# A gated mix of a spectral filter and an MLP: shorter products of zeros at the start, one operation and one transfer at the end

## The chip, the cores and the metric

The kernel runs on one core of a Trainium2 chip. The metric is the device time of one execution in microseconds (us); three runs of the kernel before took 353.65, 354.13 and 354.32 us. A profile of one execution shows what each engine did: PE (TensorE; its weight loads are listed as PEld), DVE (VectorE), ACT (ScalarE), POOL (GpSimd) and SP (SyncE, which issues most transfers). ACT and POOL issue transfers too.

## The reference

x is 2048 x 512. The result is `g * a + (1 - g) * b`, where all three come from x:

```python
g = sigmoid((x * gate_w).sum(-1, keepdims=True))
X = rfft2(x) * (w_r + 1j * w_i)      # w: 2048 x 257
a = irfft2(X, s=(2048, 512))
h = gelu(x @ w1 + b1)                # w1: 512 x 1792
b = h @ w2 + b2                      # w2: 1792 x 512
```

## The kernel before

The rows of x are taken as 16 sets of 128 (`j`), the hidden columns as 14 blocks of 128 (`f`), the output columns as 4 blocks of 128 (`q`). The 16 sets are worked on four at a time (`c`), so that one block of a result is 128 x 512.

The Fourier transform over the 512 columns is a product with tables of cosines and sines (`pd`, plain f32, `forward`), that over the 2048 rows a product of 128 (`py`) with butterflies on VectorE (`stage1`, `filt`, `stage4`); the way back is `pz` and `pa` (`inverse`). In the MLP numbers are split into two parts of 12 bits, high and low, and a product is three products in one pass each (type fp32r); sevenfold products of 2 x 2 blocks (`seven`, `down_seven`) save an eighth of them. `nu` and `ux` are the products with w1, `po` those with w2, `dx`, `dm`, `dn`, `dz` and `dl` the last ones with w2, in `down_seven`. `ph` are the first products with w1, of which the first take raw x and w1 in plain f32.

Each piece of work is a `Step` with an engine, and the order of all 2146 steps is written out in the list `ORDER`; each engine executes its own steps in that order. A second list, `SLOTS`, says for each of the 900 buffers, in the order in which the steps name them, which slot of its pool it lies in. `w` is a pool of 46 blocks of 128 x 512, `ps` are the 8 banks of PSUM, `t2k`, `ttab` and others are further pools. A buffer whose slot was held by another has to wait until that one's last reader is done; these waits are made from the order and the slots.

At the start (lines 499 to 515) VectorE sets `zero` (128 x 128, `w`, fp32r), and PE multiplies it with itself `WARM` = 9 times (`warm`, line 506), into the bank `none`, which nobody reads; the moving side repeats `zero` four times to make 512 columns. Three more products of 256 columns (`FILL`) stand between later steps. All products are issued on line 420, which is `mm`, so they are told apart by their tiles' names. The first loads of x are issued by ACT and SP. `cf`, the table of the first transform, gets four further columns on VectorE (line 547) before the first `pd`.

At the end (`down_seven`, line 1051, with `out_of`, line 1066) the eight blocks of 128 x 512 of the last two `c` are taken out of PSUM and stored. The very last one is split: `dl` k = 0 and k = 1, 256 columns each, both filled by VectorE (`plus`) and then by nine products, of which PE does those of k = 0 first. Each is copied by ACT with scale -1 into a tile `t`. For k = 0 this is one ACT operation, and SP stores it in one transfer. For k = 1 it is two ACT operations of 128 columns; the first half is stored by SP, the second by ACT itself.

## Time and profile before

| | us |
|---|---|
| median of three runs | 354.13 (353.65 to 354.32) |
| the profiled execution | 353.74 |
| its span, from the first to the last instruction | 352.0 |
| PE busy | 344.8 (98%) |
| DVE busy | 333.4 (95%) |
| ACT busy | 301.6 (86%) |
| POOL busy | 56.6 (16%) |

Busy time of PE is modelled from pipelined products that overlap, so its share says that PE always had something under way, not that it ran at its peak. The profile's chain of waits goes back from the last instruction to whatever released it; its share by engine says what set the time. A product's own duration contains its way through the array, so what one costs in a row of many is the time from its start to the next one's start. In merged rows, this is the stretch less the duration of the last one.

### The profile page before, as it was taken

The page shows a single profiled execution, that of the slowest core. Times are in us where ns is not written, and L with a number is a line of the kernel's source. Part 1 is how long each engine was busy: PE and PEld are TensorE (multiplying, and loading weights), DVE is VectorE, ACT ScalarE, POOL GpSimd, SP SyncE. Part 2 cuts the span into 40 slices and gives each one's busy share as a digit, 9 for nine tenths or more (in the row PEclk, how much of TensorE's full clock was granted, in tenths as well). Part 3 has the DMA queues.
Part 4 walks back from the last instruction along what each step waited for, and adds up shares of the span by engine and source line. Part 5 has one row for each costly group of instructions (what it writes and reads, how often), then busy time and mean ns, then how long its engine had stood idle before and what let it go on. Part 6 is the DMA issues. An engine that isn't in the chain of part 4 may idle for free.

```text
span 352.0 us, 5796 instructions
## 1 busy us (share of the span) xinstructions
PE 344.8 (98%) x1742; PEld 291.9 (83%) x1742; DVE 333.4 (95%) x700; ACT 301.6 (86%) x631; POOL 56.6 (16%) x75
## 2 busy tenths in 40 slices
PE   8999999999999999999999999999999999999993
PEld 7988888888878888888888888888888889888883
DVE  5999999899999999999999999999999999999991
ACT  4999999999999665999759885599999999999622
POOL 2012002000003100121301301000120001463420
PEclk9999999999999999999999999999999999999998
DMA  7998896847879949999999845965582547898995
GB/s 227 378 283 287 242 300 179 226 110 288 212 239 240 183 164 294 298 225 266 240 245 239 174 116 119 298 228 180 173 175 66 148 135 208 156 152 189 196 205 198
DMA packets 47719, 74.63 MB, mean 212 GB/s; under 512 B 5544, under 2 KB 18344, under 8 KB 47688
## 3 DMA queue, kind: packets, MB, share of 16 engines
q1 hardware_dynamic: 37528, 58.42, 50.6%
q0 software_dynamic: 9728, 15.51, 27.3%
q10 hardware_dynamic: 432, 0.33, 0.3%
q8 instruction: 14, 0.23, 0.3%
q14 instruction: 17, 0.14, 0.1%
HBM read 52.02 MB, written 17.31 MB: 197 GB/s over the span
## 4 chain that ended last, share of the span: by engine, by line
PE 96%; DVE 1%; DMA 1%; issue 0%; ACT 0%; DVEq 0%
PE po L420 37%; PE uxB L420 11%; PE uxA L420 9%; PE nuB L420 8%; PE nuA L420 7%; PE pd L420 4%; PE pz L420 4%; PE py L420 3%; PE pa L420 3%; PE ph L420 3%; PE dx L420 3%; DMA xf<-in_x0g 1%; PE dm L420 1%; PE dn L420 1%; PE dz L420 1%; DVE eo L593 0%
## 5 line engine op out<-in xcount | busy, mean ns | idle before, releaser
L429 ACT ACTIVATE s<-po 128x512 f32<-128x512 f32 x40 | 23.1, 597 | 3.3 <-PE po L420 3.2
L968 ACT ACTIVATE po<-s 128x512 f32<-128x512 f32 x40 | 23.7, 598 | 0.3
L836 ACT ACTIVATE sw<-y,keep 64x512 f32<-64x512 f32 x32 | 22.5, 719 | 0.6
L775 DVE TENSOR_TENSOR m<-y,wf 128x514 f32<-128x514 f32 x32 | 21.3, 690 | 0.2
L420 PE MATMUL py<-zb,tf 128*128 128x258 f32 x96 | 20.2, 291 | 0.0
L420 PE MATMUL pd<-cf,w 128*128 128x129 f32 x128 | 18.5, 276 | 0.5 <-DVE cf L547 0.5
L420 PEld LDWEIGHTS pd<-cf,w 128*128 128x128 f32 x128 | 16.8, 191 | 1.8 <-DVE cf L547 0.7
L420 PE MATMUL pz<-tg,pq 128*128 128x128 f32 x128 | 18.3, 274 | 0.0
L420 PEld LDWEIGHTS py<-zb,tf 128*128 128x128 f32 x96 | 16.1, 189 | 2.5
L420 PEld LDWEIGHTS pz<-tg,pq 128*128 128x128 f32 x128 | 17.3, 190 | 1.0
L420 PE MATMUL nuB<-xB,wB0h 128*128 128x512 f32 x56 | 17.5, 393 | 0.0
L420 PE MATMUL pa<-zb,ci 128*128 128x256 f32 x96 | 17.0, 287 | 0.0
L420 PEld LDWEIGHTS pa<-zb,ci 128*128 128x128 f32 x96 | 15.1, 188 | 2.0
L978 ACT ACTIVATE s<-po,b2t 128x512 f32<-128x512 f32 x16 | 11.0, 693 | 6.8 <-PE po L420 6.6
L420 PE MATMUL nuA<-xA,wA0h 128*128 128x512 f32 x48 | 15.0, 393 | 0.0
L632 DVE TENSOR_TENSOR zb<-pd,zb 128x256 fp32r<-128x256 f32 x32 | 13.3, 420 | 0.8 <-ACT logit L631 0.8
L652 ACT ACTIVATE y<-pys 64x257 f32<-64x257 f32 x32 | 13.3, 417 | 0.6
L596 DVE TENSOR_TENSOR w<-eo 128x256 f32<-128x256 f32 x32 | 13.1, 419 | 0.1
L593 DVE TENSOR_TENSOR eo<-xf 128x256 f32<-128x256 f32 x32 | 12.7, 419 | 0.0
L840 DVE TENSOR_TENSOR pq<-y,sw 128x256 f32<-128x256 f32 x32 | 12.5, 416 | 0.2 <-ACT sw L836 0.2
L628 ACT ACTIVATE zb<-pd 128x256 fp32r<-128x256 f32 x32 | 12.1, 392 | 0.4 <-PE pd L420 0.4
L420 PEld LDWEIGHTS nuB<-xB,wB0h 128*128 128x128 f32 x56 | 10.4, 188 | 2.0
(595 smaller groups left out, 1262.6 us busy)
## 6 DMA issues: line engine op xcount, KB each, us to landing
wf<-in_wf SPq DMA_DIRECT2D x16, 257.0 KB
xf<-in_xt SPq DMA_DIRECT2D x14, 256.0 KB, 5.0
tf<-tf SPq DMA_DIRECT2D x16, 192.0 KB, 6.1
wrA<-in_w SPq DMA_DIRECT2D x12, 256.0 KB, 4.9
xbA<-in_xc SPq DMA_DIRECT2D x8, 256.0 KB, 5.7
xbB<-in_xc SPq DMA_DIRECT2D x8, 256.0 KB, 3.4
bacc<-s SPq DMA_DIRECT2D x8, 256.0 KB, 6.3
w<-bacc POOLq DMA_DIRECT2D x8, 256.0 KB, 4.4
```

What stands on the lines that cost most here:

```text
L420: pe.matmul(ps, w, x, start=start, stop=stop, **more)
L429: a(lambda: act.activation(o.ap(), i.ap(), AF.Copy, scale=scale), n, [i], [o])
L593: v(lambda s=s, op=op: vec.tensor_tensor(eo.ap()[:, s], x.ap()[:, 0:2], x.ap()[:, 2:4], op=op), 256, [x], [(eo, s)])
L596: v(lambda s=s, op=op: vec.tensor_tensor(w.ap()[:, s], eo.ap()[:, :, 0], eo.ap()[:, :, 1], op=op), 256, [eo], [(w, s)])
L628: a(lambda c=c: act.activation(segs(xh, c), both(c), AF.Copy), 256, [ps[c]], [(xh, c)])
L632: v(lambda c=c: vec.tensor_tensor(segs(xl, c), both(c), segs(xh, c), op=ALU.subtract), 256, [ps[c], (xh, c)], [(xl, c)])
L652: a(lambda o=o, i=i: act.activation(Y[j].ap()[o:o + HP, 1], pys.ap()[i:i + HP, 1], AF.Copy), 257, [(pys, 1)], [(Y[j], 1 + k)], more=0.07)
L775: v(lambda mk=mk, k=k, y=y, w=w: vec.tensor_tensor(mk.ap(), y.ap(), w.ap()[:, k:k + 1, :ND].to_broadcast([P, 2, ND]), op=ALU.mult), 514, [ ...
L836: a(lambda sw=sw, y=y, o=o, i=i: act.activation(sw.ap()[o:o + HP], y.ap()[i:i + HP], AF.Copy, scale=keep.ap()[i:i + HP]), 512, [y, keep, * ...
L840: v(lambda sw=sw, pq_=pq_, y=y, k=k, op=op: vec.tensor_tensor(pq_.ap()[:, k], y.ap()[:, k], sw.ap()[:, 1 - k], op=op), 256, [y, TURNED[c], ...
L968: a(lambda ps=ps, n=n, o=o: act.activation(ps.ap(), o.ap()[:, n], AF.Copy), size, [o], [ps], more=0.04)
L978: a(lambda o=o, ps=ps, q=q: act.activation(o.ap(), ps.ap(), AF.Identity, bias=b2t.ap()[:, q:q + 1]), 600, [b2t, ps], [o])
```

## The change

The nine products of zeros of 512 columns become 36 of 128 columns, which go in turn to the four parts of the bank. The last 256 output columns are copied by one ACT operation and stored by one transfer on ACT's queue; SP's and one ACT operation fall away. The list `ORDER` loses its last two numbers and is otherwise the same. 424 of the 900 numbers of `SLOTS` are others.

```diff
-2103 2131 2109 2104 2110 2135 2140 2111 2136 2137 2141 2138 2142 2144 2143 2145
+2103 2131 2109 2104 2110 2135 2140 2111 2136 2137 2141 2138 2142 2143
 SLOTS = """
-0 0 0 1 2 6 9 0 0 0 0 0 0 4 1 0 0 2 3 0 6 1 0 1 5 1 4 5 4 0 1 0 2 7 2 0 3 0 0 0 0 5 0 5 3 4 2 14 12 2 12 2 3 1 5 3 6 1
+0 0 0 1 2 6 9 0 0 0 0 0 0 4 1 0 0 2 3 0 6 1 0 1 5 1 4 5 4 0 1 0 2 7 2 0 3 0 0 0 0 5 0 5 3 4 2 7 12 2 0 2 3 1 5 3 6 1
...
     def warm():
-        for _ in range(WARM):
-            mm(none.ap(), zero.ap(), bcast(zero.ap(), 4), True, True)
+        for n in range(4 * WARM):
+            mm(none.ap()[:, n % 4], zero.ap(), zero.ap(), True, True)
...
-            t = buf("w", [P, size], F32, f"t{c}{q}{n.start}", parts=2, cls="t")
+            t = buf("w", [P, size], F32, f"t{c}{q}{n.start}", cls="t")
             if k:
-                for k in range(2):
-                    s = slice(k * P, (k + 1) * P)
-                    d = slice(n.start + k * P, n.start + (k + 1) * P)
-                    a(lambda s=s: act.activation(t.ap()[:, s], ps.ap()[:, s], AF.Copy, scale=-1.0), P, [ps], [(t, k)])
-                    if k:
-                        add("act", 0.4, 2.6, lambda s=s, d=d: act.dma_start(dst[:, d], t.ap()[:, s]), [(t, k)], [], P / 680)
-                    else:
-                        store(lambda s=s, d=d: sp.dma_start(dst[:, d], t.ap()[:, s]), P / 2, [(t, k)], [])
+                copy(t, ps, size, scale=-1.0)
+                add("act", 0.4, 2.6, lambda: act.dma_start(dst[:, n], t.ap()), [t], [], size / 680)
                 return
```

## Rows read from the trace of the kernel before

**Rows 1.** The page: busy us, share of the span and instructions by engine.
```profile
PE 344.8 (98%) x1742; PEld 291.9 (83%) x1742; DVE 333.4 (95%) x700; ACT 301.6 (86%) x631; POOL 56.6 (16%) x75
```

**Rows 2.** The page: the chain that ended last, by engine.
```profile
PE 96%; DVE 1%; DMA 1%; issue 0%; ACT 0%; DVEq 0%
```

**Rows 3.** Waits of PE (without that for `zero`): us in total, times, longest.
```profile
PE pd L420 <- DVE cf L547: 0.5, 1, 0.5
```

**Rows 4.** The chain of waits, first 9 us: start, us, what.
```profile
7.72 0.09 DVE cf L547
```

**Rows 5.** Timeline of PE, first 9 us: start, us, operation, tiles, shapes, count.
```profile
1.07 4.33 PE L420 MATMUL none<-zero 128*128 128x512 f32 x10 [1.07 <-DVE zero L501]
5.24 0.60 PE L420 MATMUL ph<-xf,war 128*128 128x128 f32 x4
...
5.80 1.54 PE L420 MATMUL ph<-xf,war 128*128 128x128 f32 x12
7.86 0.94 PE L420 MATMUL pd<-cf,w 128*128 128x129 f32 x6 [0.52 <-DVE cf L547]
```

**Rows 6.** Timeline of ACT, first 9 us.
```profile
4.61 0.72 ACT L578 ACTIVATE xA<-xf 128x256 fp32r<-128x256 f32 x2 [1.44 <-DMA xf<-in_x0g]
```

**Rows 7.** Timelines of PE and PEld, single operations on zeros.
```profile
1.23 0.34 PEld L420 LDWEIGHTS none<-zero 128*128 128x128 f32 x1
...
1.66 0.63 PE L420 MATMUL none<-zero 128*128 128x512 f32 x1
...
4.22 0.63 PE L420 MATMUL none<-zero 128*128 128x512 f32 x1
```

**Rows 8.** Timeline of PE, last products of 512 and of 256 columns.
```profile
342.75 0.62 PE L420 MATMUL dz<-gx,vth 128*128 128x512 f32 x2
343.20 0.39 PE L420 MATMUL dz<-gx,vtl 128*128 128x512 f32 x1
...
345.86 0.40 PE L420 MATMUL dl<-gx,v1h 128*128 128x256 f32 x2
346.10 0.28 PE L420 MATMUL dl<-gx,v1l 128*128 128x256 f32 x1
```

**Rows 9.** Timeline of PEld, the first two and one later weight load.
```profile
7.86 0.30 PEld L420 LDWEIGHTS pd<-cf,w 128*128 128x128 f32 x2 [0.71 <-DVE cf L547]
...
8.52 0.19 PEld L420 LDWEIGHTS none<-zero 128*128 128x128 f32 x1
```

**Rows 10.** Timelines of POOL, SP, PE around 182 us; each transfer's time to landing.
```profile
174.41 1.11 POOL L414 DMA_DIRECT2D xBt<-xbB  x1
DMA to landing us min/median/max: 8.3/8.3/8.3
...
182.37 0.55 SPq L417 DMA_DIRECT2D wBsl<-su  x1
DMA to landing us min/median/max: 4.4/4.4/4.4
190.33 0.62 PE L420 MATMUL uxB<-xBt,wBsh 128*128 128x512 f32 x2
```

**Rows 11.** Timeline of ACT, from 342 us to the end.
```profile
346.06 0.38 ACT L429 ACTIVATE t<-dl 128x256 f32<-128x256 f32 x1 [0.47 <-PE dl L420]
346.42 0.45 ACT L1074 ACTIVATE t<-dl 128x128 f32<-128x128 f32 x2
346.89 0.35 ACTq L1076 DMA_DIRECT2D out<-t  x1
```

**Rows 12.** Timeline of SP, the last two stores.
```profile
346.69 0.40 SPq L1081 DMA_DIRECT2D out<-t  x1
...
347.18 0.40 SPq L1078 DMA_DIRECT2D out<-t  x1
```

**Rows 13.** Stretches at the end: length, busy by engine, granted clock, DMA share, GB/s.
```profile
347.50:348.50 1.00, 0.00 (x0) 0.00 (x0) 0.00 (x0) 0.00 (x0) 0.00 (x0) 1.00 1.05 305
...
349.00:350.00 1.00, 0.00 (x0) 0.00 (x0) 0.00 (x0) 0.00 (x0) 0.00 (x0) 0.94 0.17 42
```

## The prediction

> **What bounds the kernel now.** I read the page's busy shares first: the reader sees TensorE (PE) at 98% of the span, VectorE and ScalarE close behind [rows 1]. Since three engines look full, the chain of waits has to decide: 96% of the path that ended last is PE [rows 2]. The table of waits then says how often PE stood still for somebody else: apart from the start only once, 0.5 us for `cf`, just before 7.86 us [rows 3]. So from 7.86 us on the time is the sum of PE's products, and the change touches none of these. It touches what lies before 7.86 us, what comes after the last product at 346.4 us, and the slots (which buffer lies where) of everything between. Each is priced from its own stretch.

> **The opening, as it is.** The chain up to 7.86 us does not run through the zeros: it comes from the first load of x over VectorE's list to the copy into `cf`, which ends at 7.81 [rows 4], and only then to PE's `pd`. On PE [rows 5] the nine products of zeros and one short filler follow each other from 1.07; the first real products (`ph`) start at 5.24. ScalarE's first use of x, at 4.61, which a load released, shows that their data was there by then [rows 6], so they wait for the zeros, about half a microsecond. That costs nothing, because after the sixteen `ph` products PE stands until `cf` is there: the last of them starts at 7.06 (5.80 + 1.54 less its own 0.28), the next could start 0.11 later, at 7.17, and `pd` starts at 7.86. **The slack of the zeros is 0.69 us.** A gain there is worth nothing: VectorE sets the 7.86.

> **The opening, changed.** 9 products of 512 columns become 36 of 128: 4608 columns both times, but 36 weight loads in place of 9. Each 512-column product of zeros takes 0.43 us from start to start (1.66 to 4.22 is six of them [rows 7]): 512 columns at the lower clock of 1.2 GHz. [...]
> What a 128-column product of this kind (f32 data marked as fp32r, one pass) costs is in no row. The nearest rows are the one-pass products of 256 columns near the end: two take 0.40 us and one 0.28, so 0.12 from start to start, and 512 columns take 0.62 - 0.39 = 0.23 [rows 8]. [...] By these rows 36 products cost 36 x (107 + at most 14) ns = 3.84 to 4.35 us at the lower clock, against 3.84 us now: the zeros end 0 to 0.5 us later, inside the slack of 0.69. **I take 0.** Below nothing: at most 0, as said. Above, two ends:
> - A weight load that comes first takes 0.17 us before its product starts at the lower clock (the first at 1.07, the second load already at 1.23 [rows 7]) and 0.11 at the higher (two `pd` loads: 0.30 less one of 0.19 [rows 9]). If loads set the pace, 23 products pass by 5.1 us, the other 13 take 1.4: the zeros end at 6.5 in place of 5.07, and 1.4 - 0.69 = 0.7 us reaches `pd`.
> - The only 128-column products in the trace are plain f32 (`pd`, `ph`, `pz`), and they go twice through the array at two cycles per column: 0.11 us each time, 0.22 a product, four cycles per column. If narrow fp32r products go at that price, 36 of them are far past the slack (first rival).

> Rows 7 show that the weight load of the next product of zeros begins while one runs (1.23, while the first lasts until 1.66), and the spacing stays that of the columns. [...]

> **The slots.** 424 of the 900 entries differ (294 `w`, 122 `ps`, 8 `t2k`); the order of the steps does not. I walked both lists along the written order and asked, for each buffer, who held its slot before and when that one's last reader ended in this trace. Nearly everywhere the new predecessor is a twin with the same last reader, or done over 0.25 us ahead. The one that comes too late is the slot of `wBsl3`: its load is issued by SP at 182.37, but the new predecessor is the raw block `xbB010`, which an accumulating transfer of POOL, issued at 174.41, reads until it lands 8.3 us later, at 182.7 [rows 10]. SP would stand 0.4 us, and with it the loads behind this one. The products that read `wBsl3` belong to the group that starts at 190.33, 8 us after the load's issue, against 4.4 us for such a load: hidden, with 3 us to spare; without that cover it would cost the 0.4. Others get looser: the loads of `xf7` and `xbA101`, for one, no longer stand behind PE's `po`. That is worth nothing to PE, which from 7.86 us on waits for nobody [rows 3]. I take 0, bounds -0.2 to +0.3 (a weight load's 0.11 us exposed or hidden in two or three places).

> **The tail.** PE's last product starts at 346.10 and takes 0.28 us. Now ScalarE empties its 256 columns in two halves: 0.45 us from 346.42 [rows 11], then its queue issues one transfer at 346.89, while SP issues the other half at 347.18, since it is busy with the first half-block's store (346.69, 0.40) until then [rows 12]. Changed: one operation of 256 columns, of which the row just before gives 0.38 us, so it ends at 346.80 in place of 346.87 (-0.07), the transfer of 128 KB is issued at 346.83, and SP's last issue is gone. The last issue thus comes 0.35 us earlier (347.18 to 346.83), and the span now ends 4.8 us behind it, at 352.0. How much of the 0.35 comes through depends on the DMA engines: they are full until 348.5 (share 1.05) and nearly empty from 349 on (0.17), with only stragglers left [rows 13]. The bytes are the same. Gain at most: 0.35 plus what one store less saves SP at its last waits (I allow 0.05), -0.4. At worst the doubled piece on one queue lands later than two halves did, by the time of its 64 KB more at 305 GB/s [rows 13], so +0.2. **I take -0.15**, near the middle, because the stretch until 348.5 is full whatever is issued when, and only the stragglers move.

> **Sum.** Opening 0, slots 0, tail -0.15. The profiled execution took 353.74 us (352.0 span and 1.74 around it) and would take 353.6; the median of the three runs, 354.13, is 0.39 above it, so I add the step to that: **354.0 us**. Its own range is 353.4 (tail -0.4, slots -0.2) to 354.7 (opening +0.7 at a load's pace less what the tail gives).

> **Rivals.**
> 1. *Narrow products at the price of plain f32* (slower). 128 columns at four cycles each are 0.43 us at the lower clock, 0.22 at the higher. Nine pass by 5.1 us, 27 more take 6.0: the zeros end at 11.1, 6.0 late, 5.3 after the slack. PE is 96% of the chain, so most goes to the end; some may be caught where it now runs just behind VectorE or ScalarE: 3.5 to 5.3, time **358.4**. For: the only narrow rows have this price, and every one-pass product here has 256 columns or more. Against: 256 and 512 columns cost exactly their columns. It decides from two cycles per column on. Chance 0.16.
> [...]
> 3. *The clock rises later* (slower), because narrow products leave the array idle between them. If it rises only when real products have run as long as the zeros do now, 4 us more, these go at half pace: 2 us lost, 1.3 after the slack: **355.3**. For: in this trace the clock rose after an unbroken run of products. Against: the columns are the same. Chance 0.10.
> 4. *The end follows the last issue, and the freed waits count too*: -0.4 for the tail, -0.4 for the slots: **353.3**. Against: three engines over 86%. Chance 0.10.

> That the change does nothing at all (tail 0) lies inside the forecast.

> **How the numbers follow.** Forecast 0.58, rivals 0.16, 0.06, 0.10, 0.10. A difference under 0.2% (0.7 us) cannot be told from none here. Within it fall nearly all of the forecast and half of rival 4: 0.60; faster 0.08; slower, rivals 1 to 3 with the forecast's upper edge as a start of them, 0.32. The range 353.1 to 357.0 takes in all but the first rival and the far ends.

> **What would show it.** Right: `ph` starts at 5.2 to 5.7, `pd` still waits for `cf` and starts at 7.86; the chain up to `pd` has no zeros in it; one ScalarE operation of 256 columns of about 0.38 us stands at the end, ScalarE's queue issues its transfer about 0.7 us after PE's last product starts, and SP's last store issue is that of the first half-block. Wrong: `pd` released by PE's own order, with the zeros in the chain (rivals 1 to 3: the spacing of the 36, 0.11, 0.17, 0.28 or 0.43 us, tells which), a low clock digit in the second slice (rival 3), or a new wait on SP or PE between 180 and 190 us.

## The result, and the profile after

The changed kernel takes **358.75 us** in the median of six runs (356.35 to 359.12), the kernel before in six runs beside them 354.02 (353.53 to 355.13): a ratio of **1.0128, 95% interval 1.0107 to 1.0149**. It is 4.7 us slower. The forecast was 354.0 with a range to 357.0; the time lies outside. Five of the six runs lie between 358.36 and 359.12; one, at 356.35, is more than 2 us faster, and no trace of it was kept.

The profiled execution took 359.12 us, with a span of 357.3 against 352.0 before. On the page, busy shares look better than before, PE at 350.1 us in place of 344.8 [rows 1]; only the chain tells that something is wrong, since PE falls from 96% of it to 88% [rows 2], and the zeros (`none`) and one load (`wrA`) stand in it. Page of the kernel after, busy time and chain by engine:

```profile
PE 350.1 (98%) x1769; PEld 297.8 (83%) x1769; DVE 333.6 (93%) x700; ACT 301.7 (84%) x630; POOL 56.5 (16%) x75
...
PE 88%; ACT 6%; DMA 2%; issue 1%; DVE 1%; SPq 0%; ACTq 0%
```

The same stretch of PE's timeline as [rows 5] (start, us, operation, tiles, shapes, count):

```profile
1.07 8.26 PE L420 MATMUL none<-zero 128*128 128x128 f32 x37 [1.07 <-DVE zero L501]
9.13 1.05 PE L420 MATMUL ph<-xf,war 128*128 128x128 f32 x4
...
10.19 2.28 PE L420 MATMUL ph<-xf,war 128*128 128x128 f32 x12
12.31 0.83 PE L420 MATMUL pd<-cf,w 128*128 128x129 f32 x6
```

Three things are to be read there. The zeros stand 0.213 us apart, although each has 128 columns: that is half the 0.427 of 512 columns [rows 7], the time of 256. 36 of them take 7.7 us in place of 3.84, and `ph` starts 3.89 us later. The twelve `ph` take 2.28 us against 1.54: the first eight stand 0.21 apart, the last four 0.11, where before all twelve were 0.115 apart in the mean ((1.54 - 0.28) / 11). The record of the granted clock begins between the two paces, with 1.00 at 11.83 us (before: 5.14). And `pd` has no wait for `cf` any more: the 0.52 us are used up, and PE itself sets the time.

"Low level" stands here for the pace ahead of that record: 512 columns of zeros in 0.427 us and a `ph` every 0.21, against 0.23 [rows 8] and 0.11 behind it. That the clock makes this difference is my reading: the record has no value there, and nowhere one in GHz. The 1.2 GHz of the prediction and of some expectations is the pace of 512 columns in 0.427 us.

The chain of the kernel after, first 31 us (start, us, what), has the zeros in it, and then a load:

```profile
1.07 8.26 PE none L420 x37
9.33 0.85 PE ph L420 x4
...
23.15 6.42 DMA wrA<-in_w
...
29.60 0.63 ACT wA0h L429
```

I matched PE's products one by one with those of before and took the difference of their starts, at times of the kernel before: +3.89 us at the first `ph`, +4.45 at the first `pd`, +4.37 at 14 us, +5.62 at 30 us, and from there the same to the last product (346.10 before, 351.78 now: +5.68). Nothing of it was caught up later. The step between 26 and 30 us is this load, for which ScalarE's `wA0h` waited; behind that wait stands `g_1l` on VectorE, and for that the third group of `po` waits at 33.48. ScalarE's timeline in the kernel after, and the one wait of PE that is not for `zero` (us in total, times, longest):

```profile
27.75 0.44 ACT L648 ACTIVATE pys<-py 128x257 f32<-128x257 f32 x1
29.60 0.63 ACT L429 ACTIVATE wA0h<-wrA 128x512 fp32r<-128x512 f32 x1 [1.41 <-DMA wrA<-in_w]
```

```profile
PE po L420 <- DVE g_1l L476: 0.8, 1, 0.8
```

At the end the shape is what the change intended. ScalarE's tail in the kernel after, against [rows 11]:

```profile
351.74 0.74 ACT L429 ACTIVATE t<-dl 128x256 f32<-128x256 f32 x2 [0.48 <-PE dl L420]
352.51 0.36 ACTq L1072 DMA_DIRECT2D out<-t  x1
```

Two operations of 0.37 us, and the transfer is issued 0.73 us after the last product's start (351.78). From that start to the end of the span are 5.56 us, before 5.87. So the account of this execution is +3.9 (zeros) +0.5 (`ph` at the low level, less the slack) +1.25 (load) -0.3 (tail) = 5.4 us.

### The profile page after: what moved, and what is told of

Its sections match the earlier page's. It is cut to its first block, busy times and chain, and to the rows that moved or that the text cites. A ratio compares the mean times of both kernels' runs of the same rounds, so it can differ in the third digit from the quotient of the medians.

```text
span 357.3 us, 5824 instructions
## 1 busy us (share of the span) xinstructions
PE 350.1 (98%) x1769; PEld 297.8 (83%) x1769; DVE 333.6 (93%) x700; ACT 301.7 (84%) x630; POOL 56.5 (16%) x75
## 4 chain that ended last, share of the span: by engine, by line
PE 88%; ACT 6%; DMA 2%; issue 1%; DVE 1%; SPq 0%; ACTq 0%
PE po L420 34%; PE uxB L420 11%; PE uxA L420 9%; PE nuB L420 8%; PE nuA L420 5%; PE pz L420 4%; PE pa L420 3%; PE dx L420 3%; PE pd L420 3%; PE none L420 2%; PE py L420 2%; PE ph L420 2%; DMA wrA<-in_w 2%; ACT s L978 1%; ACT y L652 1%
## 5 line engine op out<-in xcount | busy, mean ns | idle before, releaser
L420 PEld LDWEIGHTS nuB<-xB,wB0h 128*128 128x128 f32 x56 | 10.4, 188 | 2.1
```

What stands on the lines that cost most here:

```text
L420: pe.matmul(ps, w, x, start=start, stop=stop, **more)
```

## The experiments

One kernel is named by its label throughout. "PE late" is the difference of matched starts against the kernel before; "tail" is the span's end less the start of PE's last product. Times of before beside them: 353.78 us for wide_openers, narrow_only, narrow18 and mid18; 353.29 for narrow_oldslots, cols64, weights64 and bf16_36; 353.50 for bf16_36b, bf16_72, bf16_72_oldend and no_openers; 353.58 for wide28 and mixed62. Every trace is of one execution, and the executions of one kernel spread over 0.5 to 2.9 us, so a trace need not explain its kernel's median.

### Which part of the change

wide_openers is the kernel after with the nine zeros of 512 columns put back:

```diff
-        for n in range(4 * WARM):
-            mm(none.ap()[:, n % 4], zero.ap(), zero.ap(), True, True)
+        for _ in range(WARM):
+            mm(none.ap(), zero.ap(), bcast(zero.ap(), 4), True, True)
```

> The changed kernel with its nine opening products of 512 columns back; new slots and new end stay. Theory (the opening alone costs the 4.7 us): ph starts at 5.24, pd at 7.86, the last product at about 346.1, and the span is 0.34 us shorter than before, the gain of the new end in the profile after: about 353.7 against 354.0. Rival (the slots cost part of it, the 1.25 us that the profile after loses between 22 and 30 us): about 355, with ACT or PE waiting for a wrA load near 24 us.

narrow_only is the kernel before with that edit the other way round, so old slots, old end, narrow zeros.

> The kernel before with only the opening products changed to 36 of 128 columns; old slots, old end. Theory (opening alone): zeros 0.213 us apart, ph at 9.1, the clock rises late, pd at about 12.3, and the time is that of the changed kernel plus the 0.3 of the end: about 359.0. Rival (the slots take part): 357.5 to 358, without the extra 1.25 us between 22 and 30 us.

Measured: wide_openers 353.76 us, ratio 1.0003 (0.9992 to 1.0015). With the wide opening back, the new end and the new slots together are worth nothing that can be measured, and nothing of the loss is left. narrow_only 356.72, 1.0096 (1.0082 to 1.0110), under both of the expected times: PE is 4.25 us late at 14 us and 4.32 at the end. It does not have the late load, and its tail is shorter, 4.47 us. So the opening alone costs 2.9 us, and with the other parts around it 4.7; the rest of the experiments had to find that difference too.

narrow_oldslots asks whether the slots make it: the kernel after with the list `SLOTS` of before.

> The changed kernel (36 products of 128, the new end) with the slots of the kernel before. In the profile of the changed kernel PE lost a further 1.25 us between 26 and 39 us, where ScalarE waited 1.4 us for the load of wrA at 29.6; the kernel before with the narrow opening alone did not. Theory (the new slots let loads go ahead of that one, which then lands late): without them PE stays 4.3 us behind, time 356.5 to 357.3. Rival (run to run, or the new end): the 5.6 come back, time 358.5.

Measured: 357.98, 1.0129 (1.0103 to 1.0155), near the rival's 358.5. `wA0h` waits for the load with the old slots as well, 1.0 us, so the slots are not what brings the load late. They do decide where PE pays for it: `g_1l` starts at 32.72 us here and at 32.73 in the kernel after, but here the third group of `po` goes at 32.77 without waiting for it. PE is 4.8 us late from 14 to 35 us (its clock's record begins only at 12.75), loses 0.8 more between 35 and 60 us (times of the kernel before, as above), and is 5.52 late at the end, against 5.68.

Up to their last stores narrow_only and narrow_oldslots are the same program, and only one of them shows the wait for the load. So neither slots nor end decide whether it is late.

### What sets the 0.213 us

Four kernels change only the zeros of the kernel after: half as many (narrow18), 18 of 256 columns (mid18), 36 of 64 columns (cols64), 36 of 128 columns with 64 weight columns (weights64).

```diff
+narrow18:  for n in range(2 * WARM):
+mid18:     mm(none.ap()[:, n % 2 * 2:n % 2 * 2 + 2], zero.ap(), bcast(zero.ap(), 2), True, True)
+cols64:    mm(none.ap()[:, n % 4, :64], zero.ap(), zero.ap()[:, :64], True, True)
+weights64: mm(none.ap()[:64, n % 4], zero.ap()[:, :64], zero.ap(), True, True)
```

> The changed kernel with 18 opening products of 128 columns in place of 36, so 18 x 0.213 = 3.84 us, the same stretch as nine of 512. It parts the length of the opening from the clock. Theory (both count): the zeros end at about 5.07, ph starts at about 5.3, but the clock is still at its lower level then, as in the changed kernel, where it rose 2.7 us after ph began; the 16 ph products lose about 1.2 us, of which 0.69 is slack: pd 0.5 to 0.6 late, time 354.3 to 355.5. Rival (the clock only follows the time since the first product): it rises at about 5.1, pd at 7.86, time 353.7.

> The changed kernel with 18 opening products of 256 columns. Theory (a product with its weight load takes at least 256 columns' time, whatever its columns): 18 x 0.213 = 3.84 us, hidden loads, the clock rises at about 5.1 as with 512 columns, time 353.7. Rival (weight load and columns one after the other below 512 columns): 0.32 us each, 5.8 us, zeros end at about 7.0, pd about 1.3 late or more: 355 to 356.

> The changed kernel with 36 opening products of 64 columns (128 weight columns). It is run for the spacing of the zeros at the lower clock. Theory A (a product with its weight load takes no less than 256 columns' time): 0.213 us each as with 128. Theory B (the load's 128 columns and the product's own come one after the other, below some width): (128 + 64) / 1.2 GHz = 0.160. Theory C (narrow products take two cycles per column): 0.107, or the load's pace.

> The changed kernel with 36 opening products of 128 columns, but only 64 weight columns. Spacing at the lower clock. Theory A with the load as the cause (128 weight columns take 256 cycles, so 64 take 128): 0.107. Theory A with a fixed floor: 0.213. Theory B: (64 + 128) / 1.2 GHz = 0.160. Theory C (two cycles per product column): 0.213.

PE's timeline, the zeros of cols64, of weights64 and of mid18 (the counts of the last two have one later filler in them):

```profile
1.07 7.89 PE L420 MATMUL none<-zero 128*128 128x64 f32 x36 [1.07 <-DVE zero L501]
```

```profile
1.07 4.26 PE L420 MATMUL none<-zero 128*64 128x128 f32 x37 [1.07 <-DVE zero L501]
5.17 0.60 PE L420 MATMUL ph<-xf,war 128*128 128x128 f32 x4
```

```profile
1.06 4.26 PE L420 MATMUL none<-zero 128*128 128x256 f32 x19 [1.06 <-DVE zero L501]
5.16 0.61 PE L420 MATMUL ph<-xf,war 128*128 128x128 f32 x4
...
7.57 0.83 PE L420 MATMUL pd<-cf,w 128*128 128x129 f32 x6
```

With 64 columns the zeros are still 0.213 us apart (35 spacings in 7.49 us, the 7.89 less a product's own 0.40). With 64 weight columns, and 128 columns as in the kernel after, they are 0.107 apart. With 256 columns, 0.213 again. All these spacings, and the 0.427 of 512 columns, fit one reading: what a weight load and its product cost together is the larger of two times, that of the product's columns (0.107 for 128, 0.213 for 256) and that of the load, 0.213 for 128 fp32r columns (for 64 weight columns 0.107 is only a bound from above, since the 128 product columns take that long anyway). In these runs the load of 128 fp32r columns hides under 256 columns (0.213) and 512 (0.427) completely, and under 128 only by half (0.213 in place of 0.107). bf16_72 below shows less for bf16, at most 0.053 us. Load and columns one after the other, the rival of mid18, would make 0.32 us there; the run shows 0.213.

narrow18 tests the clock. Its 18 zeros end with those of the kernel before:

```profile
1.07 4.42 PE L420 MATMUL none<-zero 128*128 128x128 f32 x19 [1.07 <-DVE zero L501]
5.29 1.06 PE L420 MATMUL ph<-xf,war 128*128 128x128 f32 x4
...
6.35 2.25 PE L420 MATMUL ph<-xf,war 128*128 128x128 f32 x12
8.44 0.50 PE L420 MATMUL pd<-cf,w 128*128 128x129 f32 x3
```

`ph` is in time, but goes at the low level until 7.86 us, where the record of the clock begins, and `pd` is 0.58 us later than before. Its time is 353.73, 1.0005 (0.9988 to 1.0023), under the 354.3 to 355.5 expected. The median hides two groups: five runs from 352.58 to 353.27, the profiled one (352.92) among them, and five from 354.20 to 355.44. In the profiled execution the half microsecond that PE was late (0.52 at its end) came back in the tail, 4.52 us. mid18, the same length at product pace, has the clock at 4.99 and PE 0.4 us early until 340 us, and is **faster than both kernels: 352.39, 0.9965 (0.9954 to 0.9976)**, 1.3 us under the expected 353.7. Where that gain lies is not shown: its profiled execution (353.35) is the slowest of its ten, with PE 0.14 us late at the end and a tail of 5.33. weights64 took 354.54 and cols64 357.9 in one execution each; in weights64 PE was 0.2 us early until 26 us, and then 0.8 late by a wait of 1.2 us for the same load of `wrA`, so a late opening is not what this wait needs.

### With a cheap weight load

bf16_36 (one execution) and bf16_36b (the same kernel, twelve) read the 36 zeros of 128 columns as bf16; bf16_72 has 72 of 64 columns; bf16_72_oldend has these in the kernel before, with the old end and slots.

```diff
+        zb16 = zero.ap().bitcast(mybir.dt.bfloat16)[:, :P]
         for n in range(4 * WARM):
-            mm(none.ap()[:, n % 4], zero.ap(), zero.ap(), True, True)
+            mm(none.ap()[:, n % 4], zb16, zb16, True, True)
```

> The changed kernel with its 36 opening products of 128 columns in bf16 in place of f32 data. If the four-byte type is what makes narrow products slow: 0.107 us each, the zeros end at about 5.0 and the clock rises at about 5.1, pd at about 7.6 to 7.9. If not: 0.213 as before, ph at 9.1.

> The kernel after with its 36 zeros of 128 columns read as bf16 (the zeros are zeros in either type), timed in rounds. In the one look at this kernel the zeros stood 0.107 us apart and ended at 4.6 us, the first product of xf came at 4.59 and the first of cf and w at 7.62, 0.24 before its place in the kernel before (7.86). Theory of the weight load (the 128 fp32r weight columns cost 0.213 us and hide under 256 product columns and more; all that the change lost it lost there): with the load made cheap the narrow opening is as good as the wide one, ratio 0.9985 to 1.001, 353.2 to 354.1 us beside 353.7. Rival, that short products as such (36 instead of 9 instructions, restarts of the clock) cost: ratio 1.005 or more.

> The same with 72 bf16 zeros of 64 columns in place of 36 of 128: 36 more PE instructions ahead of everything, for the tail. By the gaps between the kernels so far the stretch from the start of the last product to the end is 4.3 to 4.5 us where the last fetch of PE instructions over the DMA engines lies 10 us or more ahead of that product, and mostly 5.3 to 5.9 where it lies 1 to 6 us ahead. Theory F (the fetch takes the transfers' place on one DMA engine, and the last stores end later by it): 36 more instructions bring the last fetch forward (from 340.4 to about 338 or before), and the tail falls to about 4.5 us, so 1 us faster than the 36 zeros, about 352.7 us. Rival, that the tail differs between kernels by when the last products end or by chance: the fetch moves and the tail stays at 5.3 to 5.6 us; the time is that of the 36 zeros within 0.3 us. [...]

> The kernel before (old end of the last 256 columns: two ACT halves and two transfers, old slots) with the 72 bf16 zeros of 64 columns. Beside the run with the new end and the same opening it isolates end and slots. Theory (end and slots are worth nothing, as in the run with the wide opening put back, 353.76 against 353.78): the same time within 0.5 us, the tail's start within 0.3 us. Rival, that the new end is worth the 0.3 us or more that the merged operation saves on ScalarE's queue (0.45 us of a second half): this run 0.3 to 1 us slower than the one with the new end.

bf16_36b, PE's timeline, and the zeros of bf16_72 (with one later filler in the count):

```profile
1.07 4.12 PE L420 MATMUL none<-zero 128*128 128x128 bf16 x37 [1.07 <-DVE zero L501]
5.03 0.61 PE L420 MATMUL ph<-xf,war 128*128 128x128 f32 x4
...
7.71 0.94 PE L420 MATMUL pd<-cf,w 128*128 128x129 f32 x6 [0.61 <-DVE cf L548]
```

```profile
1.07 4.40 PE L420 MATMUL none<-zero 128*128 128x64 bf16 x73 [1.07 <-DVE zero L501]
```

The narrow opening is harmless once its load is cheap: the zeros are 0.107 us apart, `pd` waits for `cf` as before, PE is 0.02 us early at the end. 352.28, 0.9967 (0.9956 to 0.9978): I had expected 353.2 to 354.1. In the profiled executions (352.24 against 353.74) the gain lies in the tail, 4.38 us against 5.87. bf16_36 itself, the same kernel, took 353.25 with a tail of 5.49. The 0.107 us are a quarter of the 0.427 of 512 columns, so the 128 columns' own time. With 64 columns, in bf16_72, the zeros are 0.053 us apart (72 spacings in 3.84 us, the 4.40 less the filler's 0.56), and the next products, `ph`, still stand 0.21 apart, as at the low level. So at the low level a load of 128 bf16 columns takes 0.053 us or less, at most a quarter of the 0.213 of the fp32r load. bf16_72 took 352.78, 0.9974 (0.9963 to 0.9985), with its last fetch of instructions 14.3 us ahead of the last product and a tail of 4.29, as the theory of the fetch asked. But it was to be 1 us faster than the 36 zeros, and is half a microsecond behind bf16_36b, whose tail was already short; its PE is 0.35 late. bf16_72_oldend: 352.76, 0.9978 (0.9970 to 0.9987), tail 4.39. Old or new end makes 0.1 us of the tail and nothing of the time.

### Without zeros

no_openers takes the zeros out of the kernel after.

> The kernel after with no zeros products at all. Theory (the clock rises only after a stretch of PE work that runs at product pace; the zeros buy that rise while PE waits for data anyway): the products of xf start no earlier than when their data are there (4.3 to 5.3 us, as the kernel before has them at 5.24), they run at 1.2 GHz, and the clock rises 2 to 4 us after they begin, at 7 to 8.5 us; the first product of cf and w comes 0.5 to 1.2 us later than in the kernel before, at 8.4 to 9.1, and the whole is 0.3 to 1.5 us slower than before: 354.1 to 355.3 us. Rival, that the zeros do nothing: the first product of cf and w at 7.6 to 7.9 us and the time of the kernel before.

Measured in one execution: `ph` at 4.35, but at the low level until 9.45, later than the 7 to 8.5 expected; `pd` at 9.11, PE 1.3 us late from 14 us to the end, at the upper edge of what the theory said. The tail is 4.29, so the span, 351.7, shows none of it; the time was 354.59, with 2.85 us around the span in place of 1.74. What these are is open. The trace has the kernel's last fetch of instructions (see the late load, below) at 353.5 us, behind the last instruction; in all the others all fourteen lie within the span.

### How the loss divides, and the late load

wide28 has 28 zeros of 512 columns, which end about where the 36 narrow ones do (`ph` 0.34 us later); mixed62 has 26 narrow zeros and then 36 of 64 columns in bf16, about as long, with 26 more instructions.

```diff
+wide28:  for _ in range(28): mm(none.ap(), zero.ap(), bcast(zero.ap(), 4), True, True)
+mixed62: for n in range(26): mm(none.ap()[:, n % 4], zero.ap(), zero.ap(), True, True)
+         for n in range(36): mm(none.ap()[:, n % 4, :64], zb16, zb16[:, :64], True, True)
```

> The kernel after with 28 zeros of the old 512 columns as its opening, long enough to end where the 36 narrow ones do (9.1 us), but at product pace all the way. It splits the 4.4 us that PE was late in the kernel after into the late end of the opening and the clock. Theory: the clock rises at 5 to 6 us as in the kernel before (the narrow zeros, bound by their weight loads, left it low until 11.83), the first product of xf starts at 9.1, its 16 products run 0.11 us apart, the first product of cf and w comes at 11.0 to 11.4, and PE is 3.2 to 3.5 us late, so 356.5 to 357.3 us without a late load of wrA. Rival, that the clock rises a time after the first real work whatever the zeros were: rise near 11.8, PE 4.3 to 4.6 us late, 357.8 us or more.

> The kernel after with an opening of about the same length (26 zeros of 128 fp32r columns, 0.213 us each, then 36 bf16 zeros of 64 columns, about 0.06 us each: 5.55 + 2.2 = 7.7 us), but with 26 more PE instructions. It is for the 1.25 us that the kernel after lost on top between 26 and 30 us, where wA0h waited 1.4 us for a load of wrA issued at 23.15, 3.4 us after a fetch of PE instructions at 19.7 that held SP's issues for 2 us. Theory of the fetch: with more instructions ahead the fetch comes 4 us earlier or more, the load of wrA lands in time, PE's delay stays at its value of 14 us (4.0 to 4.5), and the last fetch moves to about 341, so 356.4 to 357.6 us. Rival, that a late opening by itself brings the loads closer together and this one late: fetch moved, wait of wA0h 1 us or more all the same, 358.2 us or more.

wide28, PE's timeline:

```profile
9.47 0.60 PE L420 MATMUL ph<-xf,war 128*128 128x128 f32 x4
...
10.03 1.50 PE L420 MATMUL ph<-xf,war 128*128 128x128 f32 x12
11.37 0.83 PE L420 MATMUL pd<-cf,w 128*128 128x129 f32 x6
```

The clock's record begins at 4.96, and from `ph` to `pd` are 1.90 us, in the kernel after 3.18. The `ph` at the low level therefore cost 1.28 us, and the late end of the zeros the other 3.2 of the 4.45 that `pd` was late. PE is 3.43 late at 14 us (3.2 to 3.5 expected). Time: 356.81, 1.0092 (1.0071 to 1.0113). It lies in the expected range by two terms that the expectation did not have: a late load, after which PE is 4.05 late, and a short tail, 4.50.

The late load: 14 times in the span of the kernel after a packet of 16 KB fetches instructions over the transfers' engines, and SP's issue next to the first of them takes 1.0 to 2.0 us in the traces, in place of 0.43. In the kernel after, the stretch 19 to 21.5 us by queue (packets, MB, share), and SP's issues:

```profile
q8 instruction: 1, 0.02, 4.1%
```

```profile
19.24 0.43 SPq L551 DMA_DIRECT2D b2t<-in_b  x1
19.72 1.97 SPq L1173 DMA_DIRECT2D wrA<-in_w  x1
21.73 0.43 SPq L495 DMA_DIRECT2D xf<-in_xt  x1
...
23.15 0.43 SPq L1173 DMA_DIRECT2D wrA<-in_w  x1
```

The load that comes late is the one of 23.15, 3.5 us behind the fetch at 19.7. Where the fetch is 3.1 to 3.6 us ahead of that load, `wA0h` waits 1.4 (after), 1.2 (weights64), 1.0 (narrow_oldslots), 0.8 us (wide28), but not in cols64 (3.4). In the eleven traces with another distance it waits 0.2 us at most. mixed62 was made to move the fetch, and did: it is at 13.0, 7.4 us ahead of the load; there is no wait, PE's delay is 3.16 at 14 us and 3.20 at the end, and the time is 355.56, 1.0060 (1.0043 to 1.0077). That is under the 356.4 I expected: the clock's record begins at 9.41, while the kernel after had it at 11.83. So the distance of the fetch goes with the late load in four traces of five, and moving it took the wait away; what spared cols64 stays open. That the fetch causes the wait is not shown. In the kernel after the load is issued 4.97 us later than before (23.15 against 18.18) where PE is 4.36 late, so only 0.6 of the 1.4 us arise at the issue; the rest lies in the 6.4 us that the load takes to land. In cols64, issued at 22.89, it is there by 28.24.

narrow_only has neither the wait for the load (its fetch is 2.8 us ahead) nor the long tail. That is 1.25 + 1.1 us in the profiled executions, and 1.8 in the medians (4.7 less 2.9): the difference that was left open above. The one run of the kernel after at 356.35 has the time that it would have without the two.

The same fetch goes with the tail. Distance of the last fetch ahead of PE's last product, and the tail, in us, worked out from the traces:

| kernel | fetch ahead | tail |
|---|---|---|
| before, wide_openers | 1.3, 1.3 | 5.87, 5.69 |
| narrow18 | 5.0 | 4.52 |
| weights64, after, cols64, bf16_36 | 5.2, 5.4, 5.6, 5.6 | 5.62, 5.56, 5.37, 5.49 |
| mid18 | 6.1 | 5.33 |
| wide28, bf16_36b | 6.2, 6.4 | 4.50, 4.38 |
| narrow_oldslots, narrow_only, mixed62 | 10.4, 11.2, 13.4 | 4.28, 4.47, 4.21 |
| bf16_72, bf16_72_oldend, no_openers | 14.3, 15.4, 25.7 | 4.29, 4.39, 4.29 |

Up to 6.1 us ahead, the tail is 5.3 to 5.9 (narrow18 aside); from 6.2 on it is 4.2 to 4.5. SP's last wait, for the stores, shows the difference: in the kernel after, in bf16_36b and in bf16_72 (us in total, times, longest):

```profile
SPq L1369 <- DMA out<-t: 3.5, 2, 2.9
```

```profile
SPq L1370 <- DMA out<-t: 2.3, 2, 1.5
```

```profile
SPq L1370 <- DMA out<-t: 2.2, 2, 1.4
```

Two of these kernels (bf16_72, mixed62) were made to move the fetch, and their tails are 4.29 (about 4.5 expected) and 4.21. Since bf16_36b has 4.38 without the move, this does not separate the fetch from chance. The spread of the times speaks for the fetch: the runs of bf16_72 and bf16_72_oldend, with the fetch far ahead, lie within 0.5 and 0.7 us, those of bf16_36b within 1.8 (ten from 351.9 to 352.7, two at 353.5 and 353.7). That the fetch's packet holds up one engine's share of the last stores is the reading that fits; it is not shown, since which engine carried what the trace does not say.

## Why the prediction was wrong

- **The step that failed is "I take 0" for the opening**, with its upper bound of 0.5 us. It rested on rows of 256 and 512 columns, 0.12 and 0.23 us apart, where no 128x128 weight load shows between the products [rows 8]. They were right, and told nothing below 256: a load that takes 256 columns' time, 0.213 us, has just room there (mid18). I read what fitted as what was free. The 14 ns that the sum adds to each product come from a pace at full speed that no run shows. Measured: 0.213 us a product, `ph` 3.89 us late. The 5.1 us up to which the sums count products at the low level is in the trace of before, where the clock's record begins at 5.14.
- **The bound by the load's pace was too low.** I took the 0.17 us between a load's start and its product's start for the load's length. The row beside it had a load of 0.34 us [rows 7], a bound from above that stood in the trace and was not used. With 0.213 from the runs and the low level throughout, the same sum gives 36 x 0.213 = 7.7 us, and that is what came.
- **Rival 1 had the nearest time, 358.4, for another reason.** Its price was 0.43 us a product, double the measured; it let the clock rise at 5.1, where it rose at 11.83, and it knew of no late load. Three errors met. Rival 2, with its chance of 0.06, is the 0.28 among the signs: 0.17 us for a load and 0.11 for the columns behind it. No run shows that price; cols64, with half the columns, has 0.213 like the kernel after.
- **The lower end of the forecast's own range, 353.4, does not follow from its terms**: 354.13 less 0.4 and 0.2 is 353.5. Nothing hangs on it.
- **Rival 3's effect was real.** The clock's record began late, at 11.83 in place of 5.14. But it was a rival by itself, with chance 0.10, while it came together with the slower zeros; I had them as alternatives. Its size was off: it gave 2 us lost, 1.3 of them behind the slack. Lost were 1.28 us with the slack already used up (wide28 against the kernel after), and 0.58 behind the slack where the load-bound zeros end in time (narrow18). That 1.3 and 1.28 are alike is luck. Its reason, an array that idles, no run shows.
- **"From 7.86 us on PE waits for nobody" held only for the order as it was.** With PE 4.4 us late the load of `wrA` came late beside an instruction fetch, 1.25 us more, and none of the delay was absorbed, where rival 1 allowed up to 1.8 to be.
- **Slots, 0: held for the time.** wide_openers has the new slots and the time of before. But with the late load the new slots make PE wait for `g_1l` (0.78 us, in the kernel after), where with the old ones it does not; that a slot can cost PE a wait it did not have before was not among the cases priced. In the end the old slots lose as much elsewhere (narrow_oldslots). The 0.4 us that SP was to stand at `wBsl3` are not there: in wide_openers SP issues it at 182.10 without a wait for the transfer of `xbB`.
- **Tail, -0.15: not contradicted.** The pair bf16_72 and bf16_72_oldend differs by 0.1 us of tail and not in time. But the tail has a swing of more than 1 us of its own, which goes with the fetch, which I had not seen in the profile, and which is larger than the whole step.
- **The signs named were the right ones but for one**: the zeros in the chain, `pd` without a wait, and the spacing, though 0.213 was none of the four values. The low digit of the clock in the second slice did not show: the page has 9 in every slice, though `ph` goes at the low level, because no record of the clock lies before 11.83.

## What to carry to other kernels

A row in which one operation hides another shows that the cover is long enough, not how much shorter it may be: before making it shorter, find the hidden one's own length, and if no row gives it, keep its recorded duration as the price. In these runs products that only keep PE busy came at their columns' price where these took at least as long as the weight load: 256 columns with a load of 128 fp32r columns (0.213 us both, mid18), but not 128 (0.213 in place of 0.107, after). With 18 products of 256 columns, or 36 of 128 in bf16, the opening cost nothing; that these kernels were 0.3% faster than before is not shown to come from the opening. Differences of a microsecond between two such kernels go with where an instruction fetch falls, and also appear between executions of one kernel, so a small gain needs a look at the tail before it is given to the edit.
